# Byte-written weight signs and weight sums on GpSimd, no plain group in the second unit, earlier chunk loads

## The chip, the core and the metric

The kernel runs on one core of one Trainium2 chip. The metric is device time in microseconds (us) of one execution, lower is better. The engines are named as the profile names them: PE is TensorE (PEld its weight loads), DVE is VectorE, ACT is ScalarE, POOL is GpSimd, SP is SyncE, which here only issues DMAs. A profile covers one execution; its "span" runs from the first to the last instruction.

## The reference

```python
sig = 1.0 / (1.0 + np.exp(-f_logit))                 # x, f_logit: (2, 6080, 256)
f = lower_bound + (1.0 - lower_bound) * sig
for t in range(S):                                   # S = 6080, a scan per batch
    h = f[:, t] * h + (1.0 - f)[:, t] * x[:, t]
    y[:, t] = h
x = y.reshape(12160, 256)
h = np.maximum(x @ w_in, 0.0); x = (h * h) @ w_out   # layer 0: 256 -> 2048 -> 256
h = x @ w_in2                                        # layer 1, the same sizes
g = np.where(h > 0.0, h, np.exp(np.minimum(h, 0.0)) - 1.0)
out = g @ w_out2
```

## The kernel before

All data is float32. TensorE multiplies numbers in a shorter form (fp32r), so each operand is split in a high part and a low part (the rest), and each block product is three matmuls: high x high, high x low, low x high (`three`, L896, for the first matrix of a layer, and L1181 for the second).

The 12160 tokens are cut in 12 units of two halves each: unit 0 has halves of 512 and 384 tokens, every other one 512 and 512. The 2048 hidden columns are cut in 8 groups of 256 (`g`). A slot is one group of one unit in one layer (`m` = 0 or 1). There are two kinds of slot:

- A **plain** slot computes one half: 4 block products, so 12 matmuls of the half's width; a group of a unit takes two of them, 24 matmuls. Its products read `xa` and `xb` (or `xc`), the parts of the scan's result.
- A **seven-product** slot computes both halves at once: 7 products, 21 matmuls, named by the digits of `PATTERN` in the order 0, 2, 5, 4, 3, 6, 1. Product 5 reads a difference of the halves in `xa`, products 4 and 3 read `xb`, 6 and 1 read `xc` (`X_OF`). The differences are made by DVE in tile `F` (`minus`, L614) and split on ACT (L542) and DVE (L545). On the side of the weights it needs four sums (`weight_sums`, L379 to L382), which are split (L400 or L402 high, L405 low), kept in DRAM (`wd`) and read back with the rest as an 896 KB `ws` tile.

Unit 0 in layer 0 is plain throughout, so that the kernel can begin before the sums exist. `PLAIN_G` groups of unit 1 are plain as well; for such a unit the parts are made piece by piece (`add_mixed_parts`, `add_later_parts`).

The weights come as 64-bit floats, two 32-bit words each. 32 chunks (8 groups x in/out x two layers) are loaded in tile `st` (512 KB) and put together: ACT takes the absolute high word, scaled (L437), and the low word as an integer of a few bits (L440); DVE shifts and ors these (`magnitude`, L443) and ors the sign bit in (`sign`, L446); ACT and DVE split the result (L474, L480). Chunks are numbered `i` in the order of their due times. `EARLY` gives the first loads a due time of their own.

The order of all instructions is written at build time by the class `Order`: every step has an engine, a planned cost, a due time and what it needs; a planner goes through model time and gives each engine the most urgent step that is ready. What it writes is fixed: each engine then runs its list strictly in order and waits on semaphores. TensorE's list is set ahead by `slots`. `LOADS` and `SCANS` say which slot of unit 0 has to have begun before a scan chunk of unit 1 is loaded (L761) or transposed (L785). The scan itself is L818 on DVE.

Of the kernel before, what the change touches and what calls it, by code (L numbers as in the profile page):

```python
# [8 lines left out]
F32 = mybir.dt.float32  # L9
F32R = mybir.dt.float32r  # L10
I32 = mybir.dt.int32
U32 = mybir.dt.uint32
AF = mybir.ActivationFunctionType
ALU = mybir.AluOpType
PSUM = bass.MemoryType.PSUM

P = 128
# [1 line left out]
CN = 256  # L19
SIZES = ((512, 384), (512, 512))  # L20
LEAD = 2
PLAIN_G = 1
TLATE = 75.0
SLATE = 2.0
GATES = 1
SQUARES = 8
GAP = 56
TURN = 0.125
RELU = 4.0
TAKE = 1.5  # L30
COLD = (1.06, 1.06)
EARLY = (-18.5,)
DUE1 = 3.0
FIRST_SLOTS = True
SPIN = (11, 16, 5)
# [11 lines left out]
START = 12.0  # L47
SCANS = (1, 2, 4, 5)
GATED = 1
LOADS = (6, 8, 10, 12)  # L50

BUFS = {
    "fs": 2, "xs": 2, "fT": 2, "xT": 1, "F0": 1, "F1": 1, "xa": 1, "xb": 1, "xc": 1, "ws": 2, "wp": 2, "r": 6, "e": 2,
# [138 lines left out]
def kernel(  # L192
# [11 lines left out]
    nc = tc.nc  # L204
# [20 lines left out]
    one = const.tile([P, P], F32, name="one")  # L225
    const.tile([P, GAP], F32, name="gap")
    pools = {"ws": ctx.enter_context(tc.tile_pool(name="ws_pool", bufs=BUFS["ws"]))}
# [20 lines left out]
    def plain(m, u, g=0):  # L248
        return m == 0 and (u == 0 or u < PLAIN and g < PLAIN_G)

# [95 lines left out]
    def dve(n, fast=False, psum=False):  # L346
        return (0.12 if psum else 0.067) + n / (1920 if fast else 960)

    def chain(due, steps):

        left = sum(st[1] + order.SLACK for st in steps)
        for e, us, what, *rest in steps:
            order.add(e, us, due - left, what, *rest)
            left -= us + order.SLACK
# [8 lines left out]
    CE = 512  # L363
# [12 lines left out]
            queue.dma_start(st.rearrange("p k e w -> p k (e w)"), v)  # L376

    def weight_sums(q, a):
        nc.vector.tensor_tensor(q[:, 0], a[:, 0], a[:, 2], op=ALU.add)  # L379
        nc.vector.tensor_tensor(q[:, 2], a[:, 1], a[:, 0], op=ALU.subtract)  # L380
        nc.vector.tensor_tensor(q[:, 1], q[:, 0], a[:, 1], op=ALU.subtract)
        nc.vector.tensor_tensor(q[:, 3], a[:, 3], q[:, 1], op=ALU.subtract)  # L382

    def plain_weights(key):

# [7 lines left out]
    def add_kept_parts(t, x, key, m, c, at, due):  # L393
# [3 lines left out]
        def high_part(e):  # L397
            t["w" + x] = new("wp", [P, 4, P], F32R)
            if e == "ACT":
                nc.scalar.activation(t["w" + x], t[x], AF.Copy)  # L400
            else:
# [22 lines left out]
    def add_weights(i, m, kind, c, due, wk=None):  # L424
        t = {}

        def load(e):
            t["st"] = new("st", [P, 2, CE // 2, 2], I32)
            load_w(nc.sync, t["st"], m, kind, c)
            sv = t["st"].rearrange("p k e w -> p (k e) w")  # L430
            t["low"], t["high"] = sv[:, :, 0], sv[:, :, 1]

        def scaled(e):
            t["a"] = raw_at(c) if m == kind == 0 else new("a", [P, 4, P])
            t["v"] = t["a"].rearrange("p q i -> p (q i)")
            t["vi"] = t["v"].bitcast(I32)
            nc.scalar.activation(t["v"], t["high"].bitcast(F32), AF.Abs, scale=2.0**-112)  # L437

        def low_bits(e):
            nc.scalar.activation(t["low"], t["low"].bitcast(U32), AF.Copy, scale=LOW_SCALE)  # L440

        def magnitude(e):
            nc.vector.scalar_tensor_tensor(t["vi"], t["vi"], 3, t["low"], op0=ALU.logical_shift_left, op1=ALU.bitwise_or)  # L443

        def sign(e):
            nc.vector.scalar_tensor_tensor(t["vi"], t["high"], -0x80000000, t["vi"], op0=ALU.bitwise_and, op1=ALU.bitwise_or)  # L446

        def sums(e):
            t["q"] = new("a", [P, 4, P])
            weight_sums(t["q"], t["a"])  # L450

        def parts():

            if kind == 0:
                return [(t["a"], ws_t[wk][:, 0], ws_t[wk][:, 1])]
            if wo[m] is None:
                wo[m] = new("wo1", [P, KF, 2, D], F32R)
            v = t["a"].rearrange("p (k e) i -> p k (e i)", k=2)
            hi, lo = (wo[m][:, 2 * c : 2 * c + 2, x, :] for x in range(2))
            if m == 0:  # L460
                return [(v, hi, lo)]

            return [
                (v[:, k].rearrange("p (a q j) -> p q a j", a=4, q=KD),
                 *(u[:, k].rearrange("p (q a j) -> p q a j", a=4, q=KD) for u in (hi, lo)))
                for k in range(2)
            ]

        def high_part(e):
            if kind == 0:  # L470
                ws_t[wk] = plain_weights(wk)
            for v, hi, _ in parts():
                if e == "ACT":
                    nc.scalar.activation(hi, v, AF.Copy)  # L474
                else:
                    nc.vector.tensor_copy(hi, v)

        def low_part(e):
            for v, hi, lo in parts():
                nc.vector.tensor_tensor(lo, v, hi.bitcast(F32), op=ALU.subtract)  # L480

        def keep(e):
            nc.sync.dma_start(wd[m][c][:, :, 0:4].bitcast(F32), ws_t[wk].bitcast(F32))

        st, a = ("st", i), ("raw", c) if m == kind == 0 else key_of("a")
        steps = [
            ["SP", 0.475, load, (), [st], None, 512],
            ["ACT", act(CE), scaled, [st], [a]],
            ["ACT", act(CE), low_bits, (), [st]],
            ["DVE", dve(CE), magnitude, [st], [a]],  # L490
            ["DVE", dve(CE), sign, [st], [a]],
        ]
        if i < len(EARLY):
            order.add(*steps[0][:2], EARLY[i], *steps[0][2:])
            del steps[0]
        if m == 1 and kind == 0:
            q = key_of("a")
            chain(due - 6.0, [*steps, ["DVE", 4 * dve(P), sums, [a], [q]]])
            add_kept_parts(t, "a", a, m, c, 0, due - 2.0)
            add_kept_parts(t, "q", q, m, c, 4, due)  # L500
            return
        w = wk if kind == 0 else ("w", m, c)
        over = [("raw", k) for k in range(KG) if m == kind == 1]
        chain(due, [
            *steps,
            ["ACT", act(CE), high_part, [a], [w, *over]],
            ["DVE", dve(CE), low_part, [a], [w]],
        ])
        if kind == 0:
            order.add("SP", 0.5, due + 16.0, keep, [w], [("wd", m, c, 0)], None, 512)  # L510

    def add_sums(c, due):

        t = {}

        def sums(e):
            t["q"] = new("a", [P, 4, P])
            weight_sums(t["q"], raw_at(c))

        q = key_of("a")  # L520
        chain(due - 4.0, [["DVE", 4 * dve(P), sums, [("raw", c)], [q]]])
        add_kept_parts(t, "q", q, 0, c, 4, due)

    def add_stream(m, u, c, due, wk):
# [15 lines left out]
    def split(src, dst, e=None):  # L540
        def high(e):
            nc.scalar.activation(dst()[:, 0], src(), AF.Copy) if e == "ACT" else nc.vector.tensor_copy(dst()[:, 0], src())  # L542

# [5 lines left out]
    def split_scaled(c, src, dst):  # L549
        def high(e):  # L550
            nc.scalar.activation(dst()[:, 0], src(), AF.Copy, scale=ga[:, c : c + 1])  # L551

# [755 lines left out]
    def begin_unit(s):  # L1308
# [12 lines left out]
        elif u in mixed and m == 0:  # L1321
            if s == (m, u, None, PLAIN_G):
                add_later_parts(u, mixed[u], s)
# [49 lines left out]
```

## Time and profile before

| | |
|---|---|
| median of 3 runs | 1967.82 us (1967.82 to 1968.0) |
| the profiled execution | 1967.67 us, its span 1965.9 us |
| PE busy | 1957.9 us, 8739 matmuls |
| ACT busy | 1624.9 us |
| DVE busy | 1504.6 us |
| POOL busy | 7.9 us, 12 instructions |
| DMA | 265.80 MB |

Engine times are of the profiled execution. A span of 1965.9 us and a time of 1967.67 us mean that 1.8 us lie around the span. Matmuls are pipelined and the ends of their rows are modelled, so it is the distance from start to start that tells how fast TensorE goes.

### The profile page before, as it was taken

Reading aid. Unit: us, or ns where it says so; the run is one execution under the profiler, and the core shown is the slowest. Engines: PE = TensorE matmul, PEld = TensorE weight load, DVE = VectorE, ACT = ScalarE, POOL = GpSimd, SP = SyncE. Lnnn points to the kernel's source line nnn. Section 1 sums busy time; section 2 is a strip of 40 time slices with the busy share of each in tenths; the row PEclk is TensorE's granted clock in tenths of the full one; section 3 lists DMA queues with packets and bytes.
Section 4 is the critical chain, followed back from the end, with each engine's and each line's share of the span. In section 5 each row is a group of like instructions: output and inputs, shape, how many; then the busy total and the mean of one; then the engine's idle time right before and its main releaser. Section 6 shows DMA issues by size and latency. Waiting matters only on the chain.

```text
span 1965.9 us, 23805 instructions
## 1 busy us (share of the span) xinstructions
PE 1957.9 (100%) x8739; PEld 1634.4 (83%) x8739; DVE 1504.6 (77%) x1938; ACT 1624.9 (83%) x2184; POOL 7.9 (0%) x12
## 2 busy tenths in 40 slices
PE   9999999999999999999999999999999999999999
PEld 8888888888888888888888888888888888888888
DVE  8998889877776876877777687687775668778686
ACT  8989899888788878888878887887887878878786
POOL 1000000000000000000000000000000000000000
PEclk9999999999999999999999999999999999999999
DMA  7775565532533433354243343324323324242332
GB/s 255 222 234 191 193 190 191 179 128 85 147 126 115 130 106 134 105 148 137 86 137 136 105 137 115 122 101 127 136 94 107 122 99 137 94 136 97 114 116 74
DMA packets 226564, 265.80 MB, mean 135 GB/s; under 512 B 151696, under 2 KB 154256, under 8 KB 226448
## 3 DMA queue, kind: packets, MB, share of 16 engines
q1 hardware_dynamic: 224448, 263.83, 41.6%
q8 instruction: 68, 1.11, 0.2%
q10 hardware_dynamic: 2000, 0.46, 0.1%
q14 instruction: 48, 0.39, 0.1%
HBM read 222.56 MB, written 41.68 MB: 134 GB/s over the span
## 4 chain that ended last, share of the span: by engine, by line
PE 99%; DVE 1%; ACT 0%; issue 0%; POOL 0%; DVEq 0%; POOLq 0%
PE a L1181 53%; PE c L896 46%; DVE F L818 0%; PE a L716 0%; DVE wo L443 0%; PE c L739 0%; DVE wo L446 0%; DVE xT L776 0%; DVE o L1220 0%; DVE F L480 0%; ACT st L440 0%; DVE ws L480 0%; ACT wo L437 0%; ACT xa L551 0%; DVE xT L753 0%
## 5 line engine op out<-in xcount | busy, mean ns | idle before, releaser
L1181 PE MATMUL a<-g,wo 128*128 128x512 f32 (+2 forms) x4608 | 1156.3, 387 | 0.0
L1181 PEld LDWEIGHTS a<-g,wo 128*128 128x128 f32 x4608 | 863.8, 188 | 171.3
L1117 ACT ACTIVATE r<-c 128x512 f32<-128x512 f32 (+1 forms) x732 | 427.1, 583 | 252.6 <-PE c L896 246.1
L944 DVE TENSOR_TENSOR g<-r,g 128x1024 fp32r<-128x1024 f32 (+2 forms) x382 | 461.6, 1208 | 139.8 <-ACT g L939 131.4
L1124 DVE TENSOR_TENSOR r<-c,r 128x512 f32<-128x512 f32 (+1 forms) x549 | 375.5, 684 | 193.4 <-PE c L896 189.7
L939 ACT ACTIVATE g<-r 128x1024 fp32r<-128x1024 f32 (+2 forms) x382 | 401.7, 1052 | 68.5 <-PE a L1181 51.8
L896 PE MATMUL c<-xa,ws 128*128 128x512 f32 (+2 forms) x1719 | 446.2, 387 | 1.0 <-DVE ws L480 0.9
L896 PEld LDWEIGHTS c<-xa,ws 128*128 128x128 f32 x1719 | 321.2, 188 | 65.7 <-DVE ws L480 1.1
L896 PE MATMUL c<-xb,ws 128*128 128x512 f32 (+2 forms) x1152 | 318.0, 386 | 0.0
L934 DVE SCALAR_TENSOR_TENSOR r<-e,r 128x1024 f32<-128x1024 f32 (+1 forms) x190 | 230.7, 1214 | 105.0 <-ACT e L931 105.0
L896 PE MATMUL c<-xc,ws 128*128 128x512 f32 (+1 forms) x1104 | 308.9, 388 | 0.0
L896 PEld LDWEIGHTS c<-xb,ws 128*128 128x128 f32 x1152 | 215.7, 188 | 42.2
L896 PEld LDWEIGHTS c<-xc,ws 128*128 128x128 f32 x1104 | 207.1, 188 | 42.1
L931 ACT ACTIVATE e<-e 128x1024 f32<-128x1024 f32 (+1 forms) x190 | 198.8, 1046 | 0.7
L928 ACT ACTIVATE e<-r 128x1024 f32<-128x1024 f32 (+1 forms) x190 | 197.0, 1041 | 0.4
L922 ACT ACTIVATE r<-r 128x1024 f32<-128x1024 f32 (+1 forms) x186 | 194.1, 1044 | 0.2
L915 ACT ACTIVATE r<-r 128x1024 f32<-128x1024 f32 x87 | 91.2, 1048 | 0.0
L614 DVE TENSOR_TENSOR F<-F 128x512 f32<-128x512 f32 (+1 forms) x92 | 62.8, 683 | 1.0
L918 ACT ACTIVATE r<-r 128x512 f32<-128x512 f32 x87 | 53.7, 617 | 0.0
L818 DVE TENSOR_TENSOR_SCAN F<-fT,F,xT 128x256 f32<-128x256 f32 x66 | 48.2, 742 | 0.7
L545 DVE TENSOR_TENSOR xa<-F,xa 128x512 fp32r<-128x512 f32 (+3 forms) x47 | 43.6, 932 | 0.4
L1220 DVE STREAM_TRANSPOSE o<-a 128x512 f32<-128x512 f32 (+1 forms) x48 | 31.2, 686 | 1.2 <-PE a L1181 1.2
(89 smaller groups left out, 621.6 us busy)
## 6 DMA issues: line engine op xcount, KB each, us to landing
ws<-wd SPq DMA_DIRECT2D x183, 896.0 KB, 4.8
xd<-o SPq DMA_DIRECT2D x46, 256.0 KB, 2.9
fs<-in_f_logit_dram SPq DMA_DIRECT2D x176, 64.0 KB, 2.3
xs<-in_x_dram SPq DMA_DIRECT2D x176, 64.0 KB, 2.5
F<-xd SPq DMA_DIRECT2D x22, 512.0 KB, 4.4
out_dram<-o SPq DMA_DIRECT2D x88, 128.0 KB, 5.3
st<-in_moe_w_in_dram SPq DMA_DIRECT2D x16, 512.0 KB, 4.6
st<-in_moe_w_out_dram SPq DMA_DIRECT2D x16, 512.0 KB, 4.7
```

Source lines behind the costliest of these rows:

```text
L614: nc.vector.tensor_tensor(f[:, to], f[:, i], f[:, k], op=ALU.subtract)
L896: nc.tensor.matmul(out, lhsT=ws[:, p, w], rhs=xs[:, r, v], start=start and q == 0, stop=stop and q == 2, skip_group_check=check,)
L915: nc.scalar.activation(r_t[0], r_t[0], AF.Relu)
L922: nc.scalar.activation(r_t[0], r_t[0], AF.Square)
L928: nc.scalar.activation(t["e"], r_t[0], AF.Relu, scale=-1.0)
L931: nc.scalar.activation(t["e"], t["e"], AF.Exp, scale=-1.0)
L934: nc.vector.scalar_tensor_tensor(r_t[0], t["e"], 1.0, r_t[0], op0=ALU.subtract, op1=ALU.max)
L939: nc.scalar.activation(g_t[s, which][:, 0], r_t[0], AF.Copy)
L944: nc.vector.tensor_tensor(g_t[s, which][:, 1], r_t[0], g_t[s, which][:, 0].bitcast(F32), op=ALU.subtract)
L1117: nc.scalar.activation(r[0][:, i], t[A], f)
L1124: nc.vector.tensor_tensor(r[:, i], t[tag], r[:, i], op=ALU.add)
L1181: nc.tensor.matmul(a, lhsT=y, rhs=v, start=begin and jj == 0 and p == 0, stop=end and jj == len(mine) - 1 and p == 2, skip_group_check=True,)
```

## The change

The sign is no longer a DVE instruction for chunks `i >= 4`: GpSimd compares the high word with zero and writes 128 or 0 in the top byte of the low word (which ACT has made a small integer), so that `magnitude` ors it in. The four weight sums run on GpSimd. `PLAIN_G` is 0, so unit 1 has seven-product slots only and its parts are made by `add_parts`. The second weights chunk has an early due time, and the chunks of unit 1 are let loose by slots 2, 4, 6, 8 of unit 0 in place of 6, 8, 10, 12.

```diff
-PLAIN_G = 1
+PLAIN_G = 0
...
+BYTES = 4
+SIGN_US = 1.8
...
-EARLY = (-18.5,)
+EARLY = (-18.5, -16.5)
...
-LOADS = (6, 8, 10, 12)
+LOADS = (2, 4, 6, 8)
...
     def weight_sums(q, a):
-        nc.vector.tensor_tensor(q[:, 0], a[:, 0], a[:, 2], op=ALU.add)
-        nc.vector.tensor_tensor(q[:, 2], a[:, 1], a[:, 0], op=ALU.subtract)
-        nc.vector.tensor_tensor(q[:, 1], q[:, 0], a[:, 1], op=ALU.subtract)
-        nc.vector.tensor_tensor(q[:, 3], a[:, 3], q[:, 1], op=ALU.subtract)
+        nc.gpsimd.tensor_tensor(q[:, 0], a[:, 0], a[:, 2], op=ALU.add)
+        nc.gpsimd.tensor_tensor(q[:, 2], a[:, 1], a[:, 0], op=ALU.subtract)
+        nc.gpsimd.tensor_tensor(q[:, 1], q[:, 0], a[:, 1], op=ALU.subtract)
+        nc.gpsimd.tensor_tensor(q[:, 3], a[:, 3], q[:, 1], op=ALU.subtract)
...
+        def sign_byte(e):
+            b = t["st"].bitcast(U8).rearrange("p k e w -> p (k e) w")[:, :, 3]
+            nc.gpsimd.tensor_scalar(b, t["high"].bitcast(F32), 0.0, 128.0, op0=ALU.is_lt, op1=ALU.mult)
...
+        if i >= BYTES:
+            steps[3:] = [["POOL", SIGN_US, sign_byte, [], [st]], ["DVE", dve(CE), magnitude, [st], [a]]]
...
-            chain(due - 6.0, [*steps, ["DVE", 4 * dve(P), sums, [a], [q]]])
+            chain(due - 6.0, [*steps, ["POOL", 2.5, sums, [a], [q]]])
...
-        chain(due - 4.0, [["DVE", 4 * dve(P), sums, [("raw", c)], [q]]])
+        chain(due - 4.0, [["POOL", 2.5, sums, [("raw", c)], [q]]])
```

On TensorE the two orders differ in one place only, the first slots of unit 1 in layer 0. Before (the plain group 0: products on `xa`, outputs of unit 0, products on `xb` and `xc`):

```order
L896 MATMUL c_1095<-xa,ws 128x512 x6
L896 MATMUL c_1112<-xa,ws 128x512 x6
L1181 MATMUL a_639<-g,wo_71 128x384 x3
L1181 MATMUL a_644<-g,wo_71 128x384 x3
L1181 MATMUL a_639<-g,wo_71 128x384 x3
L1181 MATMUL a_644<-g,wo_71 128x384 x3
L896 MATMUL c_1146<-xb,ws 128x512 x3
L896 MATMUL c_1146<-xc,ws 128x512 x3
L896 MATMUL c_1164<-xb,ws 128x512 x3
L896 MATMUL c_1164<-xc,ws 128x512 x3
```

And now, in the same place (products 0, 2, 5, 4, 3 with the same outputs between them; line numbers are 9 higher in the changed file from here on):

```order
L905 MATMUL c_1129<-xa,ws 128x512 x3
L905 MATMUL c_1139<-xa,ws 128x512 x3
L1190 MATMUL a_669<-g,wo_71 128x384 x3
L905 MATMUL c_1150<-xa,ws 128x512 x3
L905 MATMUL c_1129<-xb,ws 128x512 x3
L1190 MATMUL a_677<-g,wo_71 128x384 x3
L1190 MATMUL a_669<-g,wo_71 128x384 x3
L1190 MATMUL a_677<-g,wo_71 128x384 x3
L905 MATMUL c_1129<-xb,ws 128x512 x3
```

The group has 21 matmuls of 512 columns where it had 24, and the first products that read a difference (`c_1150`, then `c_1129<-xb`) stand right behind the first six matmuls; before, the first slot with differences was the next group's.

On GpSimd, behind the six instructions of the start-up scans (L797, now L806), there was nothing. Now its list begins like this (L453 is a sign byte, L382 to L385 are the sums of one group; `wo_256` holds the raw weights of layer 0):

```order
L453 TENSOR_SCALAR st<-st 128x512 x5
L382 TENSOR_TENSOR a<-wo_256 128x128
L383 TENSOR_TENSOR a<-wo_256 128x128
L384 TENSOR_TENSOR a<-a,wo_256 128x128
L385 TENSOR_TENSOR a<-wo_256,a 128x128
L453 TENSOR_SCALAR st<-st 128x512 x2
```

In all there are 28 sign bytes and 64 instructions of sums; up to the first difference on TensorE there are 12 sign bytes and the sums of four groups. DVE has at the place of the first sums, where it had the four sums before, only what follows them (L405 is the high part of the sums, L446 a magnitude, L408 a low part):

```order
L487 TENSOR_TENSOR F_361<-wo_256,F_361 128x512
L405 CAST wp<-a 128x512
L446 SCALAR_TENSOR_TENSOR a<-a,st 128x512
L953 TENSOR_TENSOR g<-r,g 128x1024
L487 TENSOR_TENSOR wo_71<-a,wo_71 128x2x256
L408 TENSOR_TENSOR a<-a,wp 128x512
```

The cast reads sums that GpSimd has written, and the magnitude behind it reads a sign byte.

SP's list of the first loads, before (`fs` and `xs` are scan chunks, `st` weights):

```order
L376 DMA st<-in_moe_w_in_dram 128x2x512
L728 DMA fs<-in_f_logit_dram 128x2x256
L728 DMA xs<-in_x_dram 128x2x256
L728 DMA fs<-in_f_logit_dram 128x2x256
L728 DMA xs<-in_x_dram 128x2x256
L376 DMA st<-in_moe_w_in_dram 128x2x512 x2
```

And now:

```order
L379 DMA st<-in_moe_w_in_dram 128x2x512
L737 DMA fs<-in_f_logit_dram 128x2x256
L737 DMA xs<-in_x_dram 128x2x256
L379 DMA st<-in_moe_w_in_dram 128x2x512
L737 DMA fs<-in_f_logit_dram 128x2x256
L737 DMA xs<-in_x_dram 128x2x256
L379 DMA st<-in_moe_w_in_dram 128x2x512
```

The second weights chunk now goes ahead of the third scan chunk's two loads.

## Rows read from the trace of the kernel before

**Rows 1.** The page, busy time of two engines (us, share of span, instructions)

```profile
PE 1957.9 (100%) x8739; PEld 1634.4 (83%) x8739; DVE 1504.6 (77%) x1938; ACT 1624.9 (83%) x2184; POOL 7.9 (0%) x12
```

**Rows 2.** Stretch, its us; busy of PE, PEld, DVE, ACT, POOL; clock, DMA share, GB/s

```profile
60.00:70.00 10.00, 10.00 (x51) 8.96 (x50) 9.97 (x18) 9.97 (x18) 0.00 (x0) 1.00 0.85 211
600.00:900.00 300.00, 300.00 (x1326) 248.39 (x1325) 224.94 (x279) 242.22 (x316) 0.00 (x0) 1.00 0.37 118
```

**Rows 3.** What TensorE waited for: us in total, times, longest

```profile
PE c L896 <- DVE ws L480: 0.9, 1, 0.9
PE c L896 <- DVE F L480: 0.5, 1, 0.5
PE a L739 <- DMA fs<-in_f_logit_dram: 0.4, 1, 0.4
```

**Rows 4.** TensorE in order of time at the start: start, us, what, [wait]

```profile
12.52 1.45 PE L896 MATMUL c<-xa,ws 128*128 128x256 f32 x10 [0.87 <-DVE ws L480]
14.41 0.47 PE L739 MATMUL a<-one,fs 128*128 128x128 f32 x2 [0.45 <-DMA fs<-in_f_logit_dram]
...
17.70 2.56 PE L896 MATMUL c<-xa,F 128*128 128x512 f32 x10 [0.45 <-DVE F L480]
```

**Rows 5.** TensorE and ACT, in order of time, near 24 us

```profile
24.11 0.60 ACT L1039 ACTIVATE r<-c 128x512 f32<-128x512 f32 x1
24.59 0.68 ACT L440 ACTIVATE st<-st 128x512 int32<-128x512 uint32 x1
...
24.92 2.26 PE L896 MATMUL c<-xb,F 128*128 128x384 f32 x12
```

**Rows 6.** TensorE in order of time where unit 1 begins

```profile
82.92 2.88 PE L896 MATMUL c<-xa,ws 128*128 128x512 f32 x12
85.64 2.27 PE L1181 MATMUL a<-g,wo 128*128 128x384 f32 x12
87.74 0.86 PE L896 MATMUL c<-xb,ws 128*128 128x512 f32 x3
```

**Rows 7.** GpSimd in order of time, its six tensor instructions

```profile
9.69 1.61 POOL L797 TENSOR_SCALAR e<-fT,ga,gb 128x256 f32<-128x256 f32 x2 [8.39 <-ACT fT L770]
11.67 2.35 POOL L797 TENSOR_SCALAR e<-fT,ga,gb 128x256 f32<-128x256 f32 x2 [0.37 <-ACT fT L770]
15.88 3.23 POOL L797 TENSOR_SCALAR e<-fT,ga,gb 128x128 f32<-128x128 f32 x2 [1.85 <-ACT fT L770]
```

**Rows 8.** DVE in order of time beside them

```profile
13.04 0.55 DVE L554 SCALAR_TENSOR_TENSOR xa<-F,ga,xa 128x256 fp32r<-128x256 f32 x1
...
14.72 0.47 DVE L554 SCALAR_TENSOR_TENSOR xa<-F,ga,xa 128x256 fp32r<-128x256 f32 x1
15.12 0.68 DVE L446 SCALAR_TENSOR_TENSOR wo<-st,wo 128x512 int32<-128x512 int32 x1
...
17.57 0.77 DVE L446 SCALAR_TENSOR_TENSOR wo<-st,wo 128x512 int32<-128x512 int32 x1
```

**Rows 9.** DVE in order of time, first sums and the span of the budget

```profile
25.42 0.68 DVE L480 TENSOR_TENSOR wo<-a,wo 128x512 fp32r<-128x512 f32 x1
...
51.59 0.28 DVE L379 TENSOR_TENSOR a<-wo 128x128 f32<-128x128 f32 x1
...
52.53 0.69 DVE L480 TENSOR_TENSOR ws<-wo,ws 128x512 fp32r<-128x512 f32 x1
...
83.14 0.68 DVE L545 TENSOR_TENSOR xb<-F,xb 128x512 fp32r<-128x512 f32 x1
83.75 0.68 DVE L545 TENSOR_TENSOR xc<-F,xc 128x512 fp32r<-128x512 f32 x1
...
93.97 1.22 DVE L545 TENSOR_TENSOR xb<-F,xb 128x1024 fp32r<-128x1024 f32 x1
95.10 0.95 DVE L944 TENSOR_TENSOR g<-r,g 128x768 fp32r<-128x768 f32 x1
95.97 0.69 DVE L614 TENSOR_TENSOR F<-F 128x512 f32<-128x512 f32 x1
```

## What the change should do to the time

> **What bounds the kernel now.** I read the page first: TensorE is busy in 1957.9 of 1965.9 us [rows 1]. Busy says little by itself, so I took stretches: from 60 to 70 us and from 600 to 900 us TensorE is busy all the time at a granted clock of 1.00, the upper of its two levels (2.4 GHz) [rows 2]. Then what it waited for: beyond the first instructions only three waits, 0.9, 0.5 and 0.4 us [rows 3], and the timeline puts them before 18 us [rows 4]. So behind 18 us the time is the sum of the matmuls. Their price is the distance of starts: twelve of 512 columns from 82.92 to 85.64 us, 0.227 us each [rows 6]; the next twelve, of 384 columns, take from 85.64 to 87.74 us, 0.175 us each.
>
> DVE and ACT are nearly as full in the first 100 us: 9.97 of 10 us each from 60 to 70 us, DVE 225 of 300 us later [rows 2]. They do not bound, they run ahead of TensorE by small margins. What matters is whether the change takes work off TensorE and whether it uses up a margin.
>
> **Removed from TensorE.** Unit 1's first group has 21 matmuls of 512 columns in place of 24: 3 x 0.227 = 0.68 us less. Nothing covers this, since TensorE is the engine that ends last. It is the only certain term. DVE's freed time is worth nothing by itself: no matmul behind 18 us waits for DVE.
>
> **The budget of DVE.** The price of the seven-product group is that the differences are due earlier. Unit 1's first matmul stands at 82.92 us [rows 6]. Now products 0, 2, 5 (nine matmuls, 2.04 us) and three of 384 columns (0.52 us) stand ahead of product 4, and its second matmul, which reads the low part of `xb`, is one more on: 82.92 + 2.04 + 0.52 + 0.23 = 85.7 us. Before, the split of that tile's differences ran at 93.97 us on DVE [rows 9].
>
> So I count DVE's list from the same instruction in both (the split of the first w_out chunk, 25.42 us) to that split. Before, 92 instructions end with the first `xb` split, and the next starts at 83.75 us [rows 9]. In the changed order 80 stand there. Prices are start to start: 0.61 us for 512 elements (83.14 to 83.75), 1.13 for 1024 (93.97 to 95.10), 0.87 for 768 (95.10 to 95.97), 0.94 for four sums (51.59 to 52.53) [rows 9], and for a gate of 256 elements or a cast I estimate half of the first, 0.3. The differences of the two lists:
> - away: 11 signs (-6.7), 12 instructions of sums (-2.8), two raw splits of 512 (-1.2);
> - new: two splits of 1024 (+2.3), four subtractions (+2.4), one magnitude and one low part (+1.2), one square of 1024 and two of 768 that stood on ACT (+2.9), a cast and a gate (+0.6).
>
> The sum is -1.2 us: DVE would end the `xb` split at about 82.5 us, 3.2 us before it is needed. That margin is what GpSimd may cost. The split for product 5, on `xa`, stands 3.2 us earlier in DVE's list (0.87 + 0.61 + 0.61 + 1.13) and is needed only 0.7 us earlier, so `xb` is the tight place.
>
> **What GpSimd costs.** Up to there it runs 12 sign bytes and 16 instructions of sums. The trace has neither; its nearest rows are six `TENSOR_SCALAR` of two operations [rows 7]: a pair of 256 elements took 1.61 us and another 2.35 us, a pair of 128 elements 3.23 us, so 0.8 to 1.6 us each, with no relation to size. The pairs that took long had DVE instructions with two inputs in SBUF beside them, so GpSimd waits for DVE. What DVE loses: two instructions of the same form show it, 0.55 against 0.47 us (13.04 and 14.72) and 0.77 against 0.68 us (17.57 and 15.12) [rows 8], 0.08 and 0.09 us; the other DVE rows beside GpSimd have their usual times. The low bound for 28 instructions is nothing. The high one is that DVE stands still for as long as each runs, at least 0.8 us: 22 us. I take 0.09 us each, the nearest row: 2.5 us, inside the 3.2 us.
>
> The Trainium skill speaks against the change here: "SBUF — State Buffer", section "Who interferes with whom", says that a DVE instruction with two SBUF inputs and a GpSimd instruction that reads SBUF exclude each other for a whole instruction, and whoever comes second blocks fully. Rows 7 agree with that on GpSimd's side; rows 8 show DVE delayed by 0.09 us and not by a GpSimd instruction's 0.8 us or more. By the rule in full the sum is that of the second rival below, by the rows it is mine.
>
> As to GpSimd's own lateness: 28 x 0.8 to 1.6 us is 22 to 45 us of the 60 us at hand, so it keeps up. But the order was written with 2.5 us for four sums that depend on each other, and the rows give 3.2 to 6.5 us; behind them on GpSimd stand sign bytes, and in DVE's list a cast and a magnitude wait for these. Where DVE waits, nothing holds GpSimd up, so the short price applies: 0.7 us and a little more per group, for three groups. I take half of this as hidden by what DVE has in hand, about 1 us, and 2.5 + 1 is about the margin. So I count no new wait of TensorE.
>
> **The start.** The second weights chunk is now loaded ahead of the third scan chunk. TensorE's wait of 0.45 us before 17.70 us was for that chunk's low part on DVE [rows 4], and it can vanish. But further on in its list TensorE takes a result tile that ACT frees at 24.71 us, 0.21 us before its start at 24.92 [rows 5], and in the new order ACT has the next chunk's L440 (0.68 us, now at 24.59) in front of that freeing, not behind. So what is won at 17.7 us is lost at 24.9 us. The third scan chunk's transposes stand before the first products in TensorE's list and come later, which at worst repeats the wait of 0.45 us before 14.41 us. I take 0, with 0.9 us either way (two such waits).
>
> **Sum.** 1967.67 us (the profiled execution, of which the span is 1965.9) - 0.68 + 0 = 1966.99 us. The median of the runs is 0.15 us above the profiled one, so I predict 1967.1 us.
>
> **Rivals.**
> 1. *GpSimd is late.* The sums take their contended time where DVE cannot be idle instead, 1.5 us over plan for each of three groups: 4.5 us with the 2.5 us of lost DVE time, against a margin of 3.2, is a TensorE wait of about 3.8 us at product 4; by the short price it is 1.4 us. Time 1968.5 to 1971. For it: 3.23 us for two instructions of only 128 elements. Against it: where DVE waits, the contention ends.
> 2. *DVE stands still under GpSimd*, the other side: 28 x 0.8 = 22 us less 3.2 us of margin, TensorE waits 19 us in the first 90 us, 1986 us; it decides from 0.28 us lost per GpSimd instruction on (7.8 us, of which the margin takes 3.2, the removed matmuls 0.7 and the bound below 3.9). For it: rows 7 show the exclusion. Against: rows 8.
> 3. *The start wins.* The 0.45 us at 17.7 us, and as much before, are kept: 1966.2 to 1966.7 us. For it: DVE loses no time there; against: the 0.21 us of rows 5.
> That the change does nothing on TensorE is excluded: its order has three matmuls fewer.
>
> **How the numbers follow.** My forecast, with TensorE fed as before, 0.55; GpSimd late 0.25; DVE standing still, in full or by a good part, 0.11; the start 0.08; more than that 0.01. 0.2%, which is about what a measurement of this kernel can tell from no change, is 3.9 us. Faster by more would take all waits of TensorE and more, so 0.01. Slower holds the second rival and a little of the first: 0.14. The rest, 0.85, is within. The range goes from 1966.0 (the removed matmuls and both start waits, with a little to spare) to 1971.6 us, the end of the first rival; above it lie about 0.13.
>
> **What would show it.** The matmul count is 8736. TensorE busy without gap in stretches behind 20 us would confirm the budget; a wait of `c<-xb` on DVE L554 between 85 and 92 us would be the first rival, and DVE idle with GpSimd as releaser beside it. DVE rows of 512 elements that take 1.2 us and more in place of 0.68 would be the second. The wait before 17.70 us gone and none at 25 us would be the third. I am wrong if another wait appears that I have not counted, as ACT's on sums for their high part (which ACT has for some groups) holding up the freeing of result tiles.

## The result, and the profile after

The changed kernel takes 1981.88 us (median of 6 runs, 1980.44 to 1982.35) where the kernel before takes 1967.82: a ratio of 1.007, 95% interval 1.0057 to 1.0083. It is 14 us slower, and the forecast of 1967.1 us (1966.0 to 1971.6) was wrong. The profiled execution took 1980.71 us, 13.0 us more than that of before. (A "row" below is one instruction in the profile's timeline, or several alike that it merges.)

The page of the changed kernel, busy time by engine and, from its groups of instructions, the new sign bytes (line; busy us, mean ns of one; idle time ahead of them):

```profile
PE 1963.0 (99%) x8736; PEld 1633.3 (83%) x8736; DVE 1493.4 (75%) x1849; ACT 1622.9 (82%) x2180; POOL 134.4 (7%) x104
...
L453 POOL TENSOR_SCALAR st<-st 128x512 uint8<-128x512 f32 x28 | 82.3, 2972 | 193.1 <-ACT st L443 164.1
```

TensorE has its three matmuls fewer and DVE 89 instructions fewer [rows 1], but TensorE's rows add up to 5 us more, and a sign byte takes 2.97 us in the mean where the prediction reckoned with 0.8 to 1.6. The longest waits of TensorE now (us in total, times, longest):

```profile
PE c L905 <- ACT r L1126: 2.9, 1, 2.9
PE a L1190 <- DVE g L953: 2.4, 3, 1.4
PE a L725 <- POOL one masks.py:199: 1.4, 1, 1.4
PE a L748 <- DMA fs<-in_f_logit_dram: 1.2, 1, 1.2
PE c L905 <- DVE F L487: 0.7, 2, 0.4
PE c L905 <- DVE r L1133: 0.6, 1, 0.6
```

Before, three waits stood behind the first instructions, all in the first 18 us [rows 3, 4]; now there are many behind those. How much each stretch lost can be counted without the modelled ends of matmuls: from every distance between two starts I take away the price of that width (0.227 us for 512 columns, 0.174 for 384, and so on, the medians), and add up what is left over. Before that is 9.9 us, practically all of it in the first 20 us; after it is 23.6 us. The difference, 13.7 us, less the 0.68 us of the removed matmuls is the 13.0 us of the profiled times. By stretch: 0.7 us less up to 20 us, 4.0 more from 20 to 60, 9.3 more from 60 to 105, and 1.1 more in all the rest (0.8 of it one wait at 379 us). So the loss lies in the stretch of the prediction's budget, and begins long before product 4, where the prediction looked for it. The worst place is product 4, in TensorE's rows in order of time:

```profile
92.78 0.86 PE L905 MATMUL c<-xa,ws 128*128 128x512 f32 x3
96.58 0.96 PE L905 MATMUL c<-xb,ws 128*128 128x512 f32 x3 [2.93 <-ACT r L1126]
97.38 2.89 PE L1190 MATMUL a<-g,wo 128*128 128x384 f32 x9
```

The wait is put down to ACT, which has to read the result tile that product 4 adds to. But ACT stands in line behind DVE there:

```profile
94.04 1.06 ACT L551 ACTIVATE xc<-F 128x1024 fp32r<-128x1024 f32 x1 [0.24 <-DVE F L623]
95.00 1.04 ACT L948 ACTIVATE g<-r 128x1024 fp32r<-128x1024 f32 x1
95.95 0.58 ACT L1126 ACTIVATE r<-c 128x512 f32<-128x512 f32 x1
```

Its split of `xc` waits for DVE's subtraction (L623), and the reading of the tile (L1126) comes two instructions later, ending at 96.53 us, 1.1 us behind DVE's `xb` split (95.40). So in the last 1.1 us it is this chain that holds TensorE, and no longer the `xb` split. DVE's own list tells why both are late, in order of time:

```profile
23.18 1.22 DVE L933 TENSOR_TENSOR r<-r 128x1024 f32<-128x1024 f32 x1
24.31 1.22 DVE L953 TENSOR_TENSOR g<-r,g 128x1024 fp32r<-128x1024 f32 x1
25.45 0.68 DVE L487 TENSOR_TENSOR wo<-a,wo 128x512 fp32r<-128x512 f32 x1
28.73 0.98 DVE L446 SCALAR_TENSOR_TENSOR wo<-wo,st 128x512 int32<-128x512 int32 x1 [2.60 <-POOL st L453]
29.62 1.21 DVE L933 TENSOR_TENSOR r<-r 128x1024 f32<-128x1024 f32 x1
...
37.87 1.67 DVE L933 TENSOR_TENSOR r<-r 128x1024 f32<-128x1024 f32 x1
...
87.65 1.13 DVE L623 TENSOR_TENSOR F<-F 128x512 f32<-128x512 f32 x1
...
92.19 0.94 DVE L446 SCALAR_TENSOR_TENSOR a<-a,st 128x512 int32<-128x512 int32 x1
93.05 0.95 DVE L623 TENSOR_TENSOR F<-F 128x512 f32<-128x512 f32 x1
93.93 1.47 DVE L554 TENSOR_TENSOR xb<-F,xb 128x1024 fp32r<-128x1024 f32 x1
```

From the first w_out split (25.45 us) to the end of the `xb` split (93.93 + 1.47 = 95.40) DVE needs 69.95 us; the prediction's sum was 82.5 - 25.4 = 57.1 us, and TensorE allows 85.7 - 25.4 = 60.3. Two things can be read off. In many places instructions of 512 elements take 0.94 to 1.13 us where they took 0.68, those of 1024 take 1.47 and once 1.67 where they took 1.22 [rows 9]. I compared each DVE row from 25.2 us to that split with the median of its operation and size before: 64 rows that have a GpSimd instruction beside them are 8.5 us longer in all, the 16 others 0.1 us shorter. And DVE now waits for sign bytes, from 20 to 105 us:

```profile
DVE wo L446 <- POOL st L453: 2.8, 2, 2.6
DVE a L446 <- POOL st L453: 1.4, 2, 1.2
```

That is 4.2 us. With the longer rows (8.5 less 0.1 us) it makes 12.6 of the 12.85 us by which the list is longer than reckoned. GpSimd's rows, in order of time, show its side:

```profile
22.85 5.84 POOL L453 TENSOR_SCALAR st<-st 128x512 uint8<-128x512 f32 x1 [2.88 <-ACT st L443]
...
28.52 2.69 POOL L453 TENSOR_SCALAR st<-st 128x512 uint8<-128x512 f32 x1
...
46.14 0.47 POOL L382 TENSOR_TENSOR a<-wo 128x128 f32<-128x128 f32 x1
46.56 0.93 POOL L383 TENSOR_TENSOR a<-wo 128x128 f32<-128x128 f32 x1
...
87.56 2.73 POOL L453 TENSOR_SCALAR st<-st 128x512 uint8<-128x512 f32 x1 [3.26 <-ACT st L443]
...
122.81 2.70 POOL L453 TENSOR_SCALAR st<-st 128x512 uint8<-128x512 f32 x1 [18.05 <-ACT st L443]
```

A sign byte takes 2.70 us at 122.81, when ACT's data is all it waits for, and 5.84 us at 22.85. Beside the latter, DVE's rows of two inputs at 23.18, 24.31 and 25.45 run one behind the other in their usual times, and the sign byte ends 2.56 us after the last of them (26.13 to 28.69), so it seems to have been kept out until DVE paused; and DVE paused because it was waiting for this sign byte. The next one, 28.52 to 31.21, began 0.2 us ahead of DVE's row of 28.73: that one is 0.3 us longer, and the row of 29.62 inside the same sign byte has its usual time. A DVE without a gap does not always keep a sign byte out: the one of 87.56 took 2.73 us although DVE was busy throughout (10.00 of 10 us from 80 to 90 us, below), and there DVE's row of 87.65 took 1.13 us in place of 0.68, and the next its usual time. With the sign bytes of 28.52 and 87.56 it is one DVE row that pays, the one that begins just behind the start of the sign byte. What decides which engine gives way, these rows do not show. (Spans on GpSimd are rough; these agree with the starts of what follows.) A sum takes 0.47 us or twice as long.

Last, the granted clock, which was 1.00 throughout before [rows 2] (columns: stretch, its us, busy of PE, PEld, DVE, ACT, POOL, clock, DMA share, GB/s):

```profile
80.00:90.00 10.00, 8.60 (x47) 7.83 (x46) 10.00 (x13) 7.59 (x13) 6.66 (x6) 1.00 0.52 172
90.00:100.00 10.00, 6.85 (x27) 5.60 (x26) 10.00 (x11) 6.82 (x10) 9.84 (x12) 0.88 0.63 183
100.00:120.00 20.00, 20.00 (x92) 17.16 (x92) 16.34 (x26) 17.06 (x25) 3.19 (x6) 0.97 0.68 232
```

Behind the wait of 2.93 us the clock is at its lower level, 1.2 GHz, for 3.4 us (97.6 to 101.0 us). The nine matmuls of 384 columns from 97.38 us are a part of it: 2.89 us, where nine such take 1.75 us at the upper level. All matmuls that start in those 3.4 us are together 1.5 us longer than at the upper level.

### The profile page after: what moved, and what is told of

Its sections match the earlier page's. It is cut to its first block, busy times and chain, and to the rows that moved or that the text cites. A ratio compares the mean times of both kernels' runs of the same rounds, so it can differ in the third digit from the quotient of the medians.

```text
span 1978.9 us, 23846 instructions
## 1 busy us (share of the span) xinstructions
PE 1963.0 (99%) x8736; PEld 1633.3 (83%) x8736; DVE 1493.4 (75%) x1849; ACT 1622.9 (82%) x2180; POOL 134.4 (7%) x104
## 4 chain that ended last, share of the span: by engine, by line
PE 93%; DVE 3%; issue 2%; POOL 1%; ACT 0%; DMA 0%; SPq 0%; DVEq 0%; POOLq 0%; ACTq 0%
PE a L1190 50%; PE c L905 43%; POOL st L453 1%; DVE F L827 1%; DVE g L953 0%; DVE a L446 0%; DMA fs<-in_f_logit_dram 0%; DVE wo L446 0%; DVE wo L487 0%; DVE F L623 0%; DVE r L933 0%; PE a L725 0%; DVE xT L814 0%; SPq L770 0%; DVE xa L554 0%
## 5 line engine op out<-in xcount | busy, mean ns | idle before, releaser
L1126 ACT ACTIVATE r<-c 128x512 f32<-128x512 f32 (+1 forms) x736 | 430.0, 584 | 251.9 <-PE c L905 245.5
L953 DVE TENSOR_TENSOR g<-r,g 128x1024 fp32r<-128x1024 f32 (+2 forms) x382 | 464.1, 1215 | 148.9 <-ACT g L948 140.7
L453 POOL TENSOR_SCALAR st<-st 128x512 uint8<-128x512 f32 x28 | 82.3, 2972 | 193.1 <-ACT st L443 164.1
L623 DVE TENSOR_TENSOR F<-F 128x512 f32<-128x512 f32 (+1 forms) x92 | 63.5, 691 | 1.0
L554 DVE TENSOR_TENSOR xa<-F,xa 128x1024 fp32r<-128x1024 f32 (+3 forms) x46 | 43.9, 960 | 0.4
```

The lines of the kernel that those rows point to most:

```text
L453: nc.gpsimd.tensor_scalar(b, t["high"].bitcast(F32), 0.0, 128.0, op0=ALU.is_lt, op1=ALU.mult)
L953: nc.vector.tensor_tensor(g_t[s, which][:, 1], r_t[0], g_t[s, which][:, 0].bitcast(F32), op=ALU.subtract)
L1126: nc.scalar.activation(r[0][:, i], t[A], f)
```

## The experiments

Theory 1: GpSimd's work costs DVE more than its margin, as above. Theory 2: the differences of unit 1 are due too early for DVE's list, whoever makes signs and sums. The kernel before took 1967.67 to 1967.81 us beside these runs. "List" is always DVE's time from the first w_out split to the end of the first `xb` split of unit 1, from two rows of each trace; 60.3 us is what TensorE allows.

**Signs and sums on DVE**, the rest as in the change:

```diff
-BYTES = 4
+BYTES = 99
-        nc.gpsimd.tensor_tensor(q[:, 0], a[:, 0], a[:, 2], op=ALU.add)
+        nc.vector.tensor_tensor(q[:, 0], a[:, 0], a[:, 2], op=ALU.add)
... 
-            chain(due - 6.0, [*steps, ["POOL", 2.5, sums, [a], [q]]])
+            chain(due - 6.0, [*steps, ["DVE", 4 * dve(P), sums, [a], [q]]])
```

> The changed kernel with signs and sums back on DVE: no plain group in unit 1, early loads kept. Theory 1 (GpSimd takes DVE's time): in the changed kernel DVE rows from 20 to 105 us are 9.6 us longer than the same forms before and DVE waits 4.2 us for sign bytes; without GpSimd both go, TensorE has three matmuls fewer: 1966.2 to 1967.5 us. Theory 2 (the differences of unit 1 are due too early for DVE, GpSimd or not): TensorE still waits by several us between 85 and 97 us: 1971 us or more, since DVE has 11 signs and 12 sums (9.5 us) more to do before the differences than in the changed order.

Measured: 1974.56 us, ratio 1.0035 (1.0022 to 1.0048). List 66.8 us; the prediction's own prices say 57.1 + 6.7 (signs) + 2.8 (sums) = 66.6. TensorE waits for both splits of `xa` and of `xb` (1.0 us on ACT, 1.4 on DVE for `xb`), and the clock is at its lower level for 6.8 us. This is theory 2's figure: the earlier differences, with the earlier loads, cost 6.9 us when DVE keeps all its work. They are a real burden, and DVE had to be relieved of something to pay for it.

**Only the sums on GpSimd** (`BYTES = 99` in the change):

> The changed kernel with the signs back on DVE; only the weight sums stay on GpSimd. Theory 1: no sign byte, so no DVE wait of 4.2 us; of the 9.6 us of longer DVE rows 5.0 us lay beside sums alone, against 2.8 us that the sums took on DVE: 1967 to 1970 us. Theory 2: as all on DVE, 1971 us or more.

Measured: 1974.38 us, 1.0034 (1.0021 to 1.0047), the same as with all on DVE, so theory 2's figure again. List 66.5 us: DVE gets rid of 2.8 us of sums, and 2.5 us come back (66.5 for 66.8 - 2.8). By rows it is more: in the list, those beside the 20 sums that stand there are 3.9 us longer, 0.2 us a sum, while 0.7 us of waits for ACT are gone.

**Only the signs on GpSimd** (sums on DVE as in the first diff, `BYTES = 4`):

> The changed kernel with the sums back on DVE; only the sign bytes stay on GpSimd. Theory 1: the waits for sign bytes (4.2 us) and 3.9 us of longer DVE rows stay, TensorE waits again in the first 60 us: 1970 to 1977 us. Theory 2: as the changed kernel or a little worse, 1981 to 1984 us, since the sums come back to DVE ahead of the differences.

Measured: 1978.71 us, 1.0056 (1.004 to 1.0073), between the two theories. List 69.0 us. Against all on DVE, 6.7 us of signs are gone and the list is still 2.2 us longer: the sign bytes cost DVE 8.9 us. They are the dearer half. By rows: those beside the 12 sign bytes in the list are 5.7 us longer, 0.47 us a sign byte, and DVE waits 2.9 us for sign bytes.

**GpSimd's work with the order of before** (the change with `PLAIN_G = 1`, `LOADS` and `EARLY` as before):

> Signs and sums on GpSimd as in the changed kernel, but the plain group, the later chunk loads and the one early weights load of before. Theory 1: the waits before 60 us stay (some 4 us of TensorE in the changed kernel), those at 75 to 97 us shrink since the differences are due 10 us later: 1971 to 1977 us. Theory 2: without the early differences nothing is late, 1967.5 to 1969 us.

Measured: 1977.03 us, 1.0048 (1.0033 to 1.0063). Here the differences are due as before, and it is 9.4 us slower, the upper end of what theory 1 gave. So theory 2 alone does not hold either: each half of the change costs by itself, and both draw on the same DVE list.

The second set tests that list directly.

**No GpSimd work that reads the weights**: the sign bytes are left out and the sums are replaced by zeros that GpSimd writes, so that all weights are taken as positive and the sums are nought; DVE's list is that of the change.

```diff
-        nc.gpsimd.tensor_tensor(q[:, 0], a[:, 0], a[:, 2], op=ALU.add)
-        nc.gpsimd.tensor_tensor(q[:, 2], a[:, 1], a[:, 0], op=ALU.subtract)
-        nc.gpsimd.tensor_tensor(q[:, 1], q[:, 0], a[:, 1], op=ALU.subtract)
-        nc.gpsimd.tensor_tensor(q[:, 3], a[:, 3], q[:, 1], op=ALU.subtract)
+        nc.gpsimd.memset(q, 0.0)
...
-            nc.gpsimd.tensor_scalar(b, t["high"].bitcast(F32), 0.0, 128.0, op0=ALU.is_lt, op1=ALU.mult)
+            pass
```

> The change without its GpSimd work on the weights: the sign bytes are left out (weights are taken as positive), and the four sums are replaced by zeros that GpSimd writes, so DVE's list is that of the change. Ledger theory (GpSimd's price alone broke the budget: DVE would have ended the split of xb 3.2 us ahead of TensorE): no wait of TensorE over 0.6 us behind 20 us, the clock at 1.0 throughout, 1966.2 to 1968.0 us. Rival (the differences of unit 1 are due too early for DVE's list in any case, by the run with all on DVE): a wait of 1 to 3 us for xb stays, with some us at half clock, 1970 to 1975.

Measured: 1966.94 us (10 runs, 1966.57 to 1967.27), ratio 0.9995 (0.9986 to 1.0005); the prediction's sum was 1966.99 us. All that TensorE waits for in it:

```profile
PE a L721 <- POOL one masks.py:199: 1.4, 1, 1.4
PE c L744 <- DMA fs<-in_f_logit_dram: 1.0, 1, 1.0
PE a L744 <- DMA fs<-in_f_logit_dram: 0.7, 1, 0.7
PE c L901 <- DVE F L483: 0.4, 1, 0.4
PE c L901 <- DVE xb L559: 0.3, 1, 0.3
```

None of this is behind 23 us. DVE in order of time (L483 is the w_out split, L550 the split of differences):

```profile
25.66 0.69 DVE L483 TENSOR_TENSOR wo<-a,wo 128x512 fp32r<-128x512 f32 x1
...
81.71 1.23 DVE L550 TENSOR_TENSOR xb<-F,xb 128x1024 fp32r<-128x1024 f32 x1
```

and TensorE at the same place:

```profile
84.99 0.86 PE L901 MATMUL c<-xa,ws 128*128 128x512 f32 x3
85.69 0.86 PE L901 MATMUL c<-xb,ws 128*128 128x512 f32 x3
```

The list takes 57.3 us (reckoned 57.1), the split ends at 82.94 us (82.5), and product 4 begins at 85.69 us without a wait. The clock stays at 1.00. So the margin of about 3 us was there, and GpSimd's work on the weights took it. Theory 1 holds for the change as it is.

**No plain group, and nothing else** (`PLAIN_G = 0` in the kernel before):

> The kernel before with no plain group in unit 1 and nothing else changed (signs and sums on DVE, loads and early due times as before). The run of the change with all on DVE took 1974.6 us. If the earlier differences are what costs there, this takes 1972 to 1977 us, with a wait for xb or xa of 1 us or more between 80 and 95 us; if the earlier loads were to blame for it, this is at 1967 to 1968.5 us.

Measured: 1975.43 us, 1.0038 (1.0025 to 1.0051), list 66.2 us. TensorE's longest waits:

```profile
PE c L896 <- DVE xb L545: 1.4, 1, 1.4
PE a L716 <- POOL one masks.py:199: 1.4, 1, 1.4
PE c L896 <- ACT xa L542: 1.2, 1, 1.2
PE c L896 <- DVE xa L545: 1.2, 1, 1.2
PE c L896 <- ACT xb L542: 1.0, 1, 1.0
```

The 0.68 us of matmuls costs 7.6 us when DVE is not relieved. The run with all on DVE, which has the earlier loads as well, took 0.9 us less, but the two overlap (1974.79 to 1976.24 against 1974.01 to 1974.96), so the loads' worth is not told from none here.

**The sign byte behind the magnitude** that should have used it. The weights lose their signs; GpSimd does the same work.

```diff
-            steps[3:] = [["POOL", SIGN_US, sign_byte, [], [st]], ["DVE", dve(CE), magnitude, [st], [a]]]
+            steps[3:] = [["DVE", dve(CE), magnitude, [st], [a]], ["POOL", SIGN_US, sign_byte, [], [st]]]
```

> The change, with the sign byte written behind the magnitude that should have used it, so that the signs of the weights are lost; GpSimd does the same work, and DVE never waits for a sign byte. If the lengthening of DVE's instructions beside GpSimd (9.6 us up to 105 us) is most of the loss, TensorE still waits 2 us or more for xb and the time is 1976 to 1981. If the waiting for sign bytes (4.2 us) is most of it, the wait for xb is gone and the time is 1967 to 1972.

Measured: 1977.12 us, 1.0047 (1.0032 to 1.0062), list 67.6 us. Without DVE's waits for signs 4.8 us are won; the rest stays, and TensorE's longest wait is 2.2 us. DVE's rows from 20 to 105 us are 10.7 us longer than their forms before. Not all waiting is gone: the list still holds 3.1 us of it, 2.7 for ACT's split of a w_out chunk. That goes back to GpSimd too, by another way. A sign byte that took 7.71 us (from 24.05 us) held the tile `st`, so SP could issue the next weights load only at 31.79 us, and ACT's work stood behind this load:

```profile
SPq L379 <- POOL st L453: 2.5, 1, 2.5
```

So the longer rows are the greater part, the waiting the lesser, and turning the two steps round does not remove all of the waiting.

**The planner told the price** (3.6 us for a sign byte and for four sums, in both places; the planner writes another order by it):

```diff
-SIGN_US = 1.8
+SIGN_US = 3.6
...
-            chain(due - 6.0, [*steps, ["POOL", 2.5, sums, [a], [q]]])
+            chain(due - 6.0, [*steps, ["POOL", 3.6, sums, [a], [q]]])
```

> The change, with the planner told 3.6 us for a sign byte and 3.6 us for four sums in place of 1.8 and 2.5. Theory 1a (GpSimd's instructions cost DVE time mainly because DVE waits for them, being planned too short): the waits of DVE for sign bytes and sums (about 5 us up to 105 us) shrink below 1.5 us and the time falls by 3 us or more, to 1975 to 1978.5. Theory 1b (what counts is that every DVE instruction beside GpSimd is longer, about 9.6 us up to 105 us): the waits may move, but the time stays at 1980 to 1983.

Measured: 1975.53 us, 1.0039 (1.0024 to 1.0054), list 67.6 us. Up to 105 us DVE waits 0.2 us for a sign byte and 1.0 us for a cast of sums on ACT, which itself waited 1.1 us for GpSimd; DVE's rows are 10.0 us longer, about as in the change. The clock stays at 1.00. So 6 of the 14 us came from an order made with too short a price, about 1.5 of them through the lower clock, which did not come here. About 8 come with GpSimd's work in both orders; another order was not tried.

The third set asks what DVE pays for: the number of GpSimd instructions, or the time beside them.

**Half a sign byte** (each instruction over 256 of its 512 elements; the other weights lose their sign):

```diff
-            nc.gpsimd.tensor_scalar(b, t["high"].bitcast(F32), 0.0, 128.0, op0=ALU.is_lt, op1=ALU.mult)
+            hi = t["high"].bitcast(F32)
+            nc.gpsimd.tensor_scalar(b[:, :256], hi[:, :256], 0.0, 128.0, op0=ALU.is_lt, op1=ALU.mult)
```

> The change, with each sign byte instruction over 256 of the 512 elements (the other weights lose their sign); the number and place of all instructions is that of the change. Theory A (DVE pays for the time that it runs beside GpSimd, about 0.1 us for each 0.23 to 0.27 us of its own): the sign bytes take 1.4 us alone in place of 2.7, DVE's lengthening up to 105 us falls from 9.6 to about 7 us and its waits for signs are gone, so the time is 1974 to 1976. Theory B (DVE pays a fixed price for each GpSimd instruction, as the prediction reckoned): the lengthening stays at 9 to 10 us, only the waits go, and the time is 1976 to 1978.

Measured: 1974.88 us (1973.84 to 1976.95), 1.0038 (1.0023 to 1.0053), list 65.8 us. DVE's rows are 6.9 us longer, its waits for signs 2.7 us (less, but not gone). Beside sign bytes alone the rows lose 1.1 us, where they lost 3.9; beside sums it is 5.0 in both.

**The sign byte in two instructions** of 256 elements:

```diff
+            nc.gpsimd.tensor_scalar(b[:, 256:], hi[:, 256:], 0.0, 128.0, op0=ALU.is_lt, op1=ALU.mult)
```

> The change, with each sign byte instruction cut in two of 256 elements: the same elements, 28 GpSimd instructions more. Theory A (time beside GpSimd counts): DVE's lengthening stays at 9 to 10.5 us up to 105 us, and the time is 1981 to 1984, the rise coming only from the start of the second instructions. Theory B (each GpSimd instruction has its price): the lengthening from sign bytes doubles, by 3 to 4 us, and the time is 1984.5 or more.

Measured: 1982.02 us, 1.0071 (1.0055 to 1.0088), the time of the change; list 71.0 us. GpSimd's groups:

```profile
L454 POOL TENSOR_SCALAR st<-st 128x256 uint8<-128x256 f32 x28 | 48.1, 1718 | 187.9 <-ACT st L443 158.9 <-DMA wd<-a 16.2 <-DMA fs<-in_f_logit_dram 12.8
L455 POOL TENSOR_SCALAR st<-st 128x256 uint8<-128x256 f32 x28 | 47.3, 1689 | 0.0
```

GpSimd is busy 13 us longer with them (95.4 against 82.3), and DVE's rows are 9.3 us longer against 9.6, while its waits for sign bytes are 5.6 us against 4.2. With twice the instructions and the same elements DVE's rows lose the same; with the same instructions and half the elements they lose less. So for the sign byte the price goes with the elements that GpSimd works on, not with the count of instructions by which the prediction had reckoned it. It does not carry over to another operation: a sum has a quarter of a sign byte's elements and two inputs, and cost 0.2 us against 0.47 in the two runs that have only one of them.

**The loads of before** (`LOADS = (6, 8, 10, 12)` in the change):

> The change with the scan chunks of unit 1 let loose by slots 6, 8, 10, 12 as before, all else as in the change. If the earlier loads only move DVE's and ACT's scan work about inside the first 80 us, the time is 1979 to 1984, no better than the change; if they add to the crowding, it falls below 1978.

Measured: 1985.94 us (1983.58 to 1987.39), 1.0091 (1.0076 to 1.0106), above both expectations. DVE waits 9.7 us for sign bytes up to 105 us in place of 4.2, which is more than the difference. The earlier loads help the change by 4 us; I had expected them to be neutral or harmful. Why the waiting grows with the later loads was not tried.

**The early due time alone** (`EARLY = (-18.5, -16.5)` in the kernel before):

> The kernel before with the early due time of the second weights chunk and nothing else. By the prediction's step on the start (the wait of 0.45 us before 17.7 us goes, and as much is lost where a result tile is freed later, near 25 us) the time is that of before within 0.5 us, 1967.3 to 1968.3; if the start wins, it is 1966.4 to 1967.2.

Measured: 1968.4 us (10 runs, 1967.92 to 1968.81), 1.0003 (0.9994 to 1.0013): no gain, and 0.7 us more in the medians, which the interval does not tell from none. TensorE in order of time:

```profile
22.73 1.32 PE L896 MATMUL c<-xb,ws 128*128 128x384 f32 x6 [0.29 <-DVE xb L554]
24.40 1.14 PE L896 MATMUL c<-xb,ws 128*128 128x384 f32 x5 [0.35 <-DVE xb L554]
```

What is won in the first 20 us (0.7 us) is lost here (0.64 us in these two waits), on DVE's gate of unit 0 (L554), not on ACT's freeing of a tile at 24.9 us as the prediction had it; another 0.4 us goes between 60 and 105 us.

The lists and the times stand together (all kernels without a plain group):

| kernel | list, us | over 60.3 | time, us |
|---|---|---|---|
| no GpSimd input | 57.3 | none | 1966.9 |
| half a sign byte | 65.8 | 5.5 | 1974.9 |
| no plain group alone | 66.2 | 5.9 | 1975.4 |
| sums on GpSimd | 66.5 | 6.2 | 1974.4 |
| all on DVE | 66.8 | 6.5 | 1974.6 |
| planner told | 67.6 | 7.3 | 1975.5 |
| no wait for signs | 67.6 | 7.3 | 1977.1 |
| signs on GpSimd | 69.0 | 8.7 | 1978.7 |
| the change | 70.0 | 9.7 | 1981.9 |
| sign byte in two | 71.0 | 10.7 | 1982.0 |
| loads of before | 77.9 | 17.6 | 1985.9 |

Over 1966.9 us each time is the overrun plus 1.2 to 5.3 us. In every one but two the clock fell to its lower level near product 4. Where that lasted 3.4 us it is worth 1.5 to 1.7 us; where it lasted 6.8 us (all on DVE, no plain group alone) about 2.1, since TensorE stood still in part of it; with the loads of before it came twice, 3.4 us each. It did not come in the first and in that with the planner told, where the excess over the overrun is 1.3 us.

The two kernels with lists of 67.6 us show what the excess is made of. Product 4's second matmul, the first that reads the `xb` split, starts at 93.60 us with the planner told and at 93.78 us without waits for signs, so up to there they differ by 0.2 us. Their profiled times differ by 1.8 us (1975.38 and 1977.21), and the lower clock, which came in the second only, is 1.7 us.

## Why the prediction was wrong

**The failed step is the price of GpSimd on DVE.** The prediction took 0.09 us for each of 28 GpSimd instructions, 2.5 us, and 1 us of lateness. The runs show 8.4 us of longer DVE rows and 4.2 us of waiting, 12.6 us against a margin of 3.2. Two readings led there. From rows 8 I took pairs of rows that differ by 0.08 and 0.09 us as what DVE loses, though the six GpSimd instructions beside them were of another operation, and of 128 and 256 elements. Over the 33 GpSimd instructions that stand there in the end it is 8.4 / 33 = 0.25 us each. Size explains a part: half a sign byte costs less than a whole one. It does not explain all, since a sum of 128 elements costs 0.2 us; why the six cost DVE next to nothing no run shows. And from rows 7 I took 0.8 to 1.6 us as the time of one instruction "with no relation to size", while a sign byte, which has 512 elements and writes every eighth byte, takes 2.70 us by itself and 2.69 to 5.84 us (3.2 in the mean) for the 12 up to 105 us, beside DVE. The pairs that took long were put down to DVE's rows of two inputs beside them, though the shortest pair had such rows beside it too (L446 at 9.74 us). Both bounds were in the text (0 and 22 us); the choice within them followed the nearest row in form and ignored that its size was a half or a quarter.

**The margin was right.** With no GpSimd input the list took 57.3 us (57.1 reckoned; the listed terms add up to -1.3 us, not -1.2, which changes nothing) and the time was 1966.94 us (1966.99); with all on DVE the list was 66.8 (66.6). The first step, 0.68 us for three matmuls, fits this too: that run is 0.87 us faster in the medians and no execution overlaps with one of before, but the interval of the ratio (0.9986 to 1.0005) does not tell it from no change.

**GpSimd's lateness** was put on the sums. It came from sign bytes: DVE's longest wait, 2.60 us at 28.73, is for one that DVE itself seems to have kept out. "Where DVE waits, nothing holds GpSimd up" was true, but the waiting was still the full 2.6 us of a sign byte.

**The rivals.** What happened lies between the first, GpSimd late, and the second, DVE standing still. The point from which the second decides was given as 7.8 us lost, and 12.6 us were. Yet DVE did not stand still: from 20 to 105 us half of its rows beside GpSimd keep their time (38 of 75, to within 0.05 us), and 31 of the others lose 0.2 to 0.5 us. Of the signs that I had named, the wait of `c<-xb` came at 93 us in place of 85 to 92 and was put down to ACT; DVE's rows of 512 elements took 0.94 us, which is less than the 1.2 us that I had named and more than the 0.77 that I had reckoned with.

The Trainium skill, "SBUF — State Buffer", section "Who interferes with whom", has a DVE instruction with two SBUF inputs and a GpSimd instruction that reads SBUF contend, while one that only writes does not. The run with zeros written by GpSimd agrees: 13 DVE rows beside these lost 0.4 us in all. The same section says that the one that comes second is blocked for the whole of the other's instruction. The sign byte of 22.85 us could be such a case. The one of 87.56 us is not: it took 2.73 us, though a DVE row of two inputs (L953, from 86.51 us) had come first and DVE had no gap. Nor does it fit DVE's row of 28.73 us: that lost 0.3 us to a sign byte of 2.69, not 2.5.

**The clock** was not in the sum. Behind the wait of 2.93 us TensorE ran at its lower level for 3.4 us, which is 1.5 us more.

**The start** came out at nothing where it was run alone, as predicted, but by another way than was told, so the number was right by luck.

One thing stays open. The run without GpSimd input has other numbers in its weights; that its clock stays up could be due to that in part, though two other runs that lose signs fell to the lower level like the rest.

## What to carry to other kernels

Before work goes from a nearly full DVE to GpSimd, find a row of the same operation, type, stride and size on GpSimd, and count twice: what that engine takes with DVE busy beside it, and what DVE's rows beside it lose (here 0.2 to 0.5 us in four of ten). Here signs worth 6.7 us of DVE time cost DVE 8.9 us, and sums worth 2.8 cost 2.5 (3.9 by the rows alone). A list of an engine from one fixed instruction to the one that is waited for, in start-to-start prices, foretold its end within 0.5 us; it is worth making for every deadline that a change brings forward. Where an order is written by a planner, its prices have to be measured ones: told 3.6 us in place of 1.8, it won back 6 of the 14 us.

## What the runs showed of the hardware that was not expected

- A GpSimd `TENSOR_SCALAR` with 512 float32 inputs and single bytes as output took 2.70 us by itself, 1.45 us for 256 elements (runs of half a sign byte and of the sign byte in two); DVE's `sign` on the same data took 0.68 us.
- A GpSimd sum of 128 elements took 0.46 us by itself and 0.9 us in many rows beside DVE, where DVE's row of that size takes 0.28.
- GpSimd instructions that only write (memsets in the run without GpSimd input, 13 DVE rows beside them) cost DVE next to nothing, 0.4 us in all, and that in one row.
- The clock's lower level (1.2 GHz) came behind TensorE's waits, between 88 and 105 us, in ten of the kernels here, the change among them, and gave way after 3.4 or 6.8 us. In four it did not come: the kernel before, the early due time alone, the run without GpSimd input, and the planner told the price, though that waits 1.7 us at product 4.
- Beside DVE rows that followed each other without a gap, one sign byte took 5.84 us in place of 2.70 (and one 7.71 in the run without waits for signs), another 2.73, where a DVE row took 0.45 us more instead. What decides between the two is not known.
- For the sign byte DVE's loss went with the elements: with half sign bytes its rows beside them alone lost 1.1 us in place of 3.9; with sign bytes cut in two all its rows lost 9.3 us, against 9.6.
